# A fused state-space and feed-forward layer: the last 96 feed-forward features computed with tokens stationary

## The chip, the cores and the metric

The kernel runs on one core of a Trainium2 chip. The metric is the device time of one execution in microseconds. Engines are called by their profile names: PE (matrix multiplications), PEld (the loading of a stationary operand, shown beside PE), DVE (elementwise vector work), ACT (activation functions, also used for copies and scalings), POOL (small vector work), SP (here it only issues DMA transfers).

A multiplication on PE has a stationary operand (the kernel's `lhsT`, at most 128 contraction rows by 128 columns) and a moving operand (`rhs`, up to 512 columns here). The result has one partition for each stationary column and one element for each moving column. It goes to PSUM, which this kernel treats as eight banks of 128 partitions by 512 floats.

## The reference

`x` has 2048 tokens of 512 values. After a layer norm the same `xn` goes to two branches, whose outputs are added to `x`:

```python
xn = _layernorm(x)
# branch A: a diagonal complex recurrence over the tokens
dt = exp(log_dt); Lam_bar = exp(dt * Lam)
B_bar = ((Lam_bar - 1.0) / Lam)[:, None] * Bmat
Bu = einsum("bld,pd->blp", xn, B_bar)
h = Lam_bar * h + Bu[:, t, :]            # for each token t
yA = 2.0 * einsum("blp,dp->bld", hseq, Cmat).real + xn * Dskip
# branch B: a gated feed-forward layer, F = 1376 features
yB = (silu(xn @ w_gate) * (xn @ w_up)) @ w_down
out = x + yA + yB
```

F = 1376 is ten tiles of 128 features and one of 96. The change concerns this last tile of 96.

## The kernel before

**Chunks.** The 2048 tokens are worked in four chunks of 512, numbered 0 to 3. A chunk has these parts:

- Layer norm. Chunks 0 and 1 on DVE with a power on POOL (`ln_tile`), chunks 2 and 3 on ACT with a Newton iteration for the inverse square root on DVE (`ln_chunk_act`, four rounds of three small instructions, L550 to L552).
- `xnT`, the chunk with the 512 inputs on partitions: four token tiles of 128 by four input tiles. Chunk 0 is brought there by PE, chunks 1 to 3 by one DMA transposition each (`xTd1` to `xTd3`). There are two buffers, by `c % 2`.
- Gate and up products (`ffn_mm`, L760): for each of the eleven feature tiles four multiplications, one for each input tile. The weights are stationary (128 columns, 96 for the last tile), the 512 tokens move, so features come out on partitions. In chunk 0 the first six gate tiles are done in quarters of 128 tokens instead (L787). ACT takes the gate bank through SiLU into `sg` (L773, L812) and copies the up bank to `uf` (L824); DVE multiplies them into `hT` (L826), which is again stationary-ready: features on partitions, tokens along the row.
- State-space input products (`ssm_b_unit`, L840): four units, each of two banks filled by four multiplications; ACT copies them to `u_sb` (L847, L849); DVE rotates them, runs the scan and rotates back into `hss` (`ssm_elem_chunk`, L870 to L894).
- Down and output products (`dc_chunk`): four banks, one for 128 tokens each. Each first gets eleven multiplications of `hT` by `wd` (L925), then eight of `hss` by the prepared output weights `W12` (L938). Between these two groups PE does the input products of the chunk after next (the `mid` argument). DVE adds `x` (L945) and SP stores the result.

**Order.** PE and SP work strictly in the order in which the program adds their tasks. ACT, DVE and POOL get theirs from a list scheduler that runs while the kernel is built (`_schedule`), by estimated times and priorities, so their order can move when any task changes; on the chip each engine still works its list in order and waits on semaphores. PE's order is: quarters of chunk 0, the rest of the feed-forward part of chunk 0, input products of chunks 0 and 1, feed-forward part of chunk 1, down products of chunk 0, input products of chunk 2, output products of chunk 0, feed-forward part of chunk 2, and so on; chunk 3 has no further input products to put between.

**Banks.** `next_bank` gives out the bank whose last use is oldest.

**DMA order.** Nearly all transfers are issued by SP. A transposition waits for all transfers before it (in `dma`), and every ordinary transfer waits for the last transposition before it, so transpositions run alone. SP's order: the first tiles of `x`, the gate and up weights, four more tiles of `x`; then the transpositions of B (`ld_bre`, `ld_bim` into `BT`) and `xTd1`; then the last eight tiles of `x` and the skip vector `dsk` (`loads_x`); then the transpositions of C (into `hss[:, 1]`, which is free until chunk 1 needs it) and `wd` (`loads_stage_b2`); then `xTd2`, the stores of chunk 0, `xTd3`, and the other stores. `dsk` is used by `resid_chunk` (L617, L619).

Of the kernel before, what the change touches and what calls it, by code (L numbers as in the profile page):

```python
# [251 lines left out]
def bass_parallel_sum__ssm_conv_s5__swiglu_ffn__prompt_kernel(  # L252
# [32 lines left out]
    with es:  # L285
        block = es.enter_context(nc.Block())

        def sb(name, shape, dt):
            return es.enter_context(nc.sbuf_tensor(name, shape, dt))
# [8 lines left out]
        NXN = 8  # L298
        xn_sb = sb("xn_sb", [128, NXN, D], B16)
        xnT = sb("xnT", [128, 2, 4, KT, 128], B16)  # L300
        wg = sb("wg", [128, KT, Fh], B16)
        wu = sb("wu", [128, KT, Fh], B16)
        wd = sb("wd", [128, FT, D], B16)
        BT = sb("BT", [128, 2, KT, P], B16)
        W12 = sb("W12", [128, 2, PT, D], B16)
# [60 lines left out]
                return pb16[rows, b, cols]  # L366
        ptr = _PT()

        bank_ctr = [0]
        bank_state = {}  # L370

        def _bank_live(b):
            lw = g.last_w.get(("bk", b, 0))
            rd = g.readers.get(("bk", b, 0), ())
            return lw is not None and lw.eng == "pe" and len(rd) == 0 and not lw.name.startswith("pe_warm")

        bank_given = {}

        def next_bank():
            best = None  # L380
            for b in range(NB):
                if _bank_live(b):
                    continue
                key = max([bank_given.get(b, -1)] + [r.idx for h in range(2) for r in g.readers.get(("bk", b, h), ())])
                if best is None or key < best[0]:
                    best = (key, b)
            assert best is not None, "all PSUM banks live"
            bank_given[best[1]] = len(g.tasks)
            return best[1]

        next_tr = next_bank
# [12 lines left out]
        def dma(name, dst, src, writes, nbytes, reads=(), after=(), out_=False, eng="sp", xpose=False, prio=0.0, **kw):  # L404
            after = tuple(after)
            if xpose:
                after = after + tuple(dma_tasks)
                fn = lambda e, dst=dst, src=src: e.dma_start_transpose(out=dst, in_=src)
                est, nb = 2000.0, int(nbytes * 1.45)
            else:  # L410
                if xp_state[0] is not None:
                    after = after + (xp_state[0],)
                fn = lambda e, dst=dst, src=src: e.dma_start(dst, src, **kw)
                est, nb = 330.0 + nbytes / 900.0, nbytes
            t = g.add(eng, fn, reads=reads, writes=writes, name=name, dma=True, after=after, out=out_, est=est, nbytes=nb, prio=prio)
            dma_tasks.append(t)
            if xpose:
                xp_state[0] = t
            return t
# [19 lines left out]
        dma("ld_x4", x_sb[:, 4:8, :], x_v[:, 4:8, :], [("x", a) for a in range(4, 8)], 4 * TILEB)  # L439

        def loads_stage_b1():
            dma("ld_bre", BT[:, 0], A_B_re, [("BT", 0, kt) for kt in range(KT)], 512 * 512 * 2, xpose=True)
            dma("ld_bim", BT[:, 1], A_B_im, [("BT", 1, kt) for kt in range(KT)], 512 * 512 * 2, xpose=True)

        def loads_x():
            dma("ld_x8", x_sb[:, 8:12, :], x_v[:, 8:12, :], [("x", a) for a in range(8, 12)], 4 * TILEB)
            dma("ld_x12", x_sb[:, 12:16, :], x_v[:, 12:16, :], [("x", a) for a in range(12, 16)], 4 * TILEB)
            dma("ld_dsk", dsk[:], A_Dskip.partition_broadcast(128), [("dsk",)], 128 * 1024)

        def loads_stage_b2():  # L450
            dma("ld_cre", CT[:, 0], A_C_re, [("CT", 0)], 512 * 512 * 2, xpose=True)
# [10 lines left out]
              writes=[("iot",)], name="iota", est=1000)  # L462
        g.add("pool", lambda e: e.memset(halfpi[:], math.pi / 2.0), writes=[("halfpi",)], name="halfpi", est=100)
        g.add("pool", lambda e: e.memset(car[:, 0], 0.0), writes=[("car", 0)], name="car0", est=100)
        g.add("pool", lambda e: e.memset(ecst[:], math.e), writes=[("ecst",)], name="ecst", est=100)
        g.add("act", lambda e: e.activation(out=sm[:, NSM - 1, :], in_=mhalf[:, 0:PT], func=AF.Silu), reads=[("mhalf",)], writes=[("sm", "_warm")],
              name="act_warm", est=220, prio=1e6)
# [65 lines left out]
        def ln_chunk_act(c):  # L533
            A = range(4 * c, 4 * c + 4)
            cs = slice(4 * c, 4 * c + 4)
            for a in A:
                g.add("act", lambda e, a=a: e.activation(out=junk[:], in_=x_sb[:, a, :], func=AF.Identity, scale=-1.0 / D, accum_out=nmr[:, a:a + 1]),
                      reads=[("x", a)], writes=[("nmean", a), ("junk",)], name="lsum%d" % a, est=620)
                g.add("act", lambda e, a=a: e.activation(out=junk[:], in_=x_sb[:, a, :], func=AF.Square, bias=nmr[:, a:a + 1], accum_out=ve[:, a:a + 1]),
                      reads=[("x", a), ("nmean", a)], writes=[("ss", a), ("junk",)], name="lsq%d" % a, est=710)  # L540
            V, Y, T, M = ve[:, cs], rstd[:, cs], lnt[:, 0, :], nmr[:, cs]
            SS, V_, Y_, T_, NM = [("ss", a) for a in A], [("lv", c)], [("ly", c)], [("lt",)], [("nmean", a) for a in A]

            def d(nm, fn, rd, wr):
                g.add("dve", fn, reads=rd, writes=wr, name="%s%d" % (nm, c), est=75)
            d("lv", lambda e: e.tensor_scalar(out=V, in0=V, scalar1=1.0 / D, scalar2=EPS, op0=ALU.mult, op1=ALU.add), SS, V_)
            d("li", lambda e: e.tensor_scalar(out=T.bitcast(I32), in0=V.bitcast(I32), scalar1=1, scalar2=None, op0=ALU.logical_shift_right), V_, T_)
            d("ly", lambda e: e.tensor_scalar(out=Y.bitcast(I32), in0=T.bitcast(I32), scalar1=-1.0, scalar2=1597463007.0, op0=ALU.mult, op1=ALU.add), T_, Y_)
            for k in range(4):
                d("na%d" % k, lambda e: e.tensor_tensor(out=T, in0=Y, in1=Y, op=ALU.mult), Y_, T_)  # L550
                d("nb%d" % k, lambda e: e.scalar_tensor_tensor(out=T, in0=T, scalar=-0.5, in1=V, op0=ALU.mult, op1=ALU.mult), T_ + V_, T_)
                d("nc%d" % k, lambda e: e.scalar_tensor_tensor(out=Y, in0=T, scalar=1.5, in1=Y, op0=ALU.add, op1=ALU.mult), T_ + Y_, Y_)  # L552
            d("nm", lambda e: e.tensor_tensor(out=V, in0=M, in1=Y, op=ALU.mult), NM + Y_, V_)
            for a in A:
                g.add("act", lambda e, a=a: e.activation(out=xn_sb[:, a % NXN, :], in_=x_sb[:, a, :], func=AF.Identity, scale=rstd[:, a:a + 1], bias=ve[:, a:a + 1]),
                      reads=[("x", a)] + V_ + Y_, writes=[("xn", a % NXN)], name="xn%d" % a, est=620)

        def XN(c, j):
            return [("xnT", c % 2, j, 0), ("xnT", c % 2, j, 1)]
# [50 lines left out]
        def xt_chunk_dma(c):  # L610
            s0 = (4 * c) % NXN
            dma("xTd%d" % c, xnT[:, c % 2].rearrange("p j k t -> p (j k) t"), xn_sb[:, s0:s0 + 4, :],
                XNC(c), 4 * TILEB, reads=[("xn", s0 + j) for j in range(4)], xpose=True, prio=(_CFG["prio_xt"] if c > 1 else 0.0))
# [153 lines left out]
        def ffn_gate(c, i):  # L767
            fs = fsz[i]
            bk = ffn_mm(c, i, "g")
            sl = gctr[0] % NG  # L770
            gctr[0] += 1
            sg_slot[(c, i)] = sl
            g.add("act", lambda e, sl=sl, bk=bk, fs=fs: e.activation(out=sg[0:fs, sl, :], in_=pbank[0:fs, bk, :], func=AF.Silu),  # L773
                  reads=BK(bk), writes=[("sg", sl)], name="silu%d_%d" % (c, i), est=490)
# [40 lines left out]
        def ffn_up(c, i):  # L815
# [12 lines left out]
            else:  # L828
                g.add("dve", lambda e, sl=sl, bk=bk, fs=fs, i=i, hb=hb: e.tensor_tensor(out=hT[0:fs, hb, i, :], in0=sg[0:fs, sl, :], in1=pbank[0:fs, bk, :], op=ALU.mult),
                      reads=[("sg", sl)] + BK(bk), writes=[("hT", hb, i)], name="hmulp%d_%d" % (c, i), est=660, after=aH)  # L830

        usctr = [0]
        uctr = [0]

# [18 lines left out]
        def ssm_b_chunk(c):  # L853
            return [ssm_b_unit(c, pt) for pt in range(PT)]
# [101 lines left out]
        ln_chunk(1)  # L956
        loads_stage_b1()
        xt_chunk_dma(1)
        loads_x()
        loads_stage_b2()  # L960
        for i in range(0, 6):
            ffn_up(0, i)
        for i in range(6, FT):
            ffn_gate(0, i)
        for i in range(6, FT):
            ffn_up(0, i)
        units = []
        u0 = ssm_b_chunk(0)
# [4 lines left out]
            wprep_C(pt)  # L973
        u1 = ssm_b_chunk(1)
        ssm_elem_chunk(1, u1)
        for i in range(FT):
            ffn_gate(1, i)
            ffn_up(1, i)
        resid_chunk(1)
        ln_chunk(3)  # L980
        xt_chunk_dma(2)
        dc_chunk(0, mid=lambda: units.append(ssm_b_chunk(2)))
        ssm_elem_chunk(2, units[-1])
        for i in range(FT):
            ffn_gate(2, i)
            ffn_up(2, i)
        xt_chunk_dma(3)
        dc_chunk(1, mid=lambda: units.append(ssm_b_chunk(3)))
        ssm_elem_chunk(3, units[-1])
        for i in range(FT):  # L990
            ffn_gate(3, i)
            ffn_up(3, i)
        resid_chunk(2)
        resid_chunk(3)
        dc_chunk(2)
# [61 lines left out]
```

## Time and profile before

| what | value |
|---|---|
| median of 3 runs | 181.74 us (181.73 to 182.13) |
| the profiled execution, its own time | 181.75 us |
| its span, first to last instruction | 180.0 us |
| around the span | 1.75 us |
| granted PE clock | 1.0 throughout |
| multiplications, of all kinds | 910 |
| of these with 96 feature columns stationary (gate and up, last tile) | 32 |
| slowest engines by busy share | PE 98%, DVE 91%, ACT 57% |

The profile is of one execution. "Span" is the time from the first to the last instruction; the rest of the execution's time lies before and after. A busy PE in the page counts overlapping multiplications as one stretch, and the duration that the page gives for one multiplication includes the time to drain; the pace of a stream is read from the start of one group to the start of the next.

### The profile page before, as it was taken

To read this page: it belongs to the slowest core of one execution; us is meant where nothing else is said; L and a number is where in the kernel's file an instruction comes from. 1 tells how busy PE (TensorE), PEld (TensorE's weight loads), DVE (VectorE), ACT (ScalarE), POOL (GpSimd) and SP (SyncE) were. 2 spreads that over 40 slices of the span, in tenths; PEclk is the share of its full clock that TensorE was granted. 3 is DMA by queue.
4 is the path that set the end of the run, shared out by engine and by line. 5 is a ranking of instruction groups with operands and counts; after the bars stand their busy time and mean duration, and the time that the engine had idled before them with its cause. 6 is when DMAs were issued, how large, how long until landed. Compare 5 with 4: busy or idle time off the path is not lost.

```text
span 180.0 us, 2560 instructions
## 1 busy us (share of the span) xinstructions
PE 175.7 (98%) x910; PEld 85.0 (47%) x910; DVE 164.2 (91%) x354; ACT 101.7 (57%) x195; POOL 12.5 (7%) x34
## 2 busy tenths in 40 slices
PE   8899999999999999999999999999999999999994
PEld 3684444444444444444444544444444444444643
DVE  3797868999899889999999999999989999999993
ACT  3299989999999899872666600630666720000000
POOL 3531500000000610000000000000000000000000
PEclk9999999999999999999999999999999999999999
DMA  4994465666905300002340000002000000000112
GB/s 131 336 376 73 92 133 107 234 117 117 299 15 33 88 0 0 0 2 76 82 79 2 0 0 4 0 0 87 29 0 4 0 2 0 0 0 33 57 59 87
DMA packets 23396, 12.38 MB, mean 69 GB/s; under 512 B 15096, under 2 KB 23384, under 8 KB 23384
## 3 DMA queue, kind: packets, MB, share of 16 engines
q1 hardware_dynamic: 23360, 12.23, 26.0%
q8 instruction: 7, 0.11, 0.3%
q14 instruction: 5, 0.04, 0.1%
q10 hardware_dynamic: 24, 0.00, 0.0%
HBM read 6.46 MB, written 2.10 MB: 48 GB/s over the span
## 4 chain that ended last, share of the span: by engine, by line
PE 93%; DVE 2%; DMA 1%; POOL 1%; ACT 1%; issue 0%; DVEq 0%
PE pb L760 39%; PE pb L925 21%; PE pb L938 15%; PE pb L840 15%; PE pb L787 2%; DMA x_sb<-in_A_x_dram 1%; DVE st L505 1%; POOL rstd L511 1%; POOL sm L664 1%; ACT scrC L713 0%; DVE xn_sb L515 0%; DVE mv L507 0%; ACT xnT L606 0%; DVE osb L945 0%; DVE ve L509 0%
## 5 line engine op out<-in xcount | busy, mean ns | idle before, releaser
L760 PE MATMUL pb<-xnT,wu 128*128 128x512 bf16 (+1 forms) x176 | 43.7, 379 | 0.0
L879 DVE TENSOR_TENSOR_SCAN vq<-sm,car,vq 128x512 bf16<-128x512 f32 x32 | 39.5, 1270 | 0.1
L925 PE MATMUL pb<-wd,hT 128*128 128x512 bf16 (+3 forms) x187 | 38.7, 366 | 0.0
L760 PE MATMUL pb<-xnT,wg 128*128 128x512 bf16 (+1 forms) x152 | 38.4, 379 | 0.0
L773 ACT ACTIVATE sg<-pb 128x512 bf16<-128x512 f32 (+1 forms) x38 | 22.7, 596 | 15.3 <-PE pb L760 14.7
L824 ACT ACTIVATE uf<-pb 128x512 bf16<-128x512 f32 (+1 forms) x44 | 26.0, 603 | 7.3 <-PE pb L760 5.7
L938 PE MATMUL pb<-W,hss 128*128 128x512 bf16 (+1 forms) x136 | 28.3, 366 | 0.0
L840 PE MATMUL pb<-xnT,BT 128*128 128x512 bf16 x128 | 28.1, 379 | 0.0
L925 PEld LDWEIGHTS pb<-wd,hT 128*128 128x128 bf16 (+1 forms) x187 | 18.3, 98 | 19.9
L760 PEld LDWEIGHTS pb<-xnT,wu 128*128 128x128 bf16 (+1 forms) x176 | 17.6, 100 | 20.1
L760 PEld LDWEIGHTS pb<-xnT,wg 128*128 128x128 bf16 (+1 forms) x152 | 15.3, 101 | 17.6
L938 PEld LDWEIGHTS pb<-W,hss 128*128 128x128 bf16 x136 | 13.3, 98 | 14.4
L826 DVE TENSOR_TENSOR hT<-sg,uf 128x512 bf16<-128x512 bf16 (+1 forms) x44 | 18.1, 416 | 1.9 <-ACT uf L824 1.4
L840 PEld LDWEIGHTS pb<-xnT,BT 128*128 128x128 bf16 x128 | 12.5, 98 | 15.1
L847 ACT ACTIVATE u_sb<-pb 128x512 bf16<-128x512 f32 x16 | 9.5, 596 | 11.1 <-PE pb L840 10.7
L945 DVE TENSOR_TENSOR osb<-pb,x_sb 128x512 bf16<-128x512 f32 (+1 forms) x17 | 11.1, 655 | 1.5 <-PE pb L938 1.3
L870 DVE TENSOR_TENSOR scrA<-u_sb,cosT 128x1024 bf16<-128x1024 bf16 x16 | 10.9, 681 | 0.8 <-ACT u_sb L849 0.8
L885 DVE TENSOR_TENSOR scrA<-vq,cosT 128x1024 bf16<-128x1024 bf16 x16 | 11.0, 685 | 0.0
L889 DVE TENSOR_TENSOR scrA<-vq,sin 128x1024 bf16<-128x1024 bf16 x16 | 10.9, 684 | 0.0
L873 DVE TENSOR_TENSOR scrA<-u_sb,sin 128x1024 bf16<-128x1024 bf16 x16 | 10.9, 684 | 0.0
L875 DVE TENSOR_TENSOR vq<-scrA 128x1024 bf16<-128x1024 bf16 x16 | 10.5, 684 | 0.1
L894 DVE TENSOR_TENSOR hss<-scrA 128x1024 bf16<-128x1024 bf16 x16 | 10.4, 684 | 0.0
(79 smaller groups left out, 135.2 us busy)
## 6 DMA issues: line engine op xcount, KB each, us to landing
out_dram<-osb SPq DMA_DIRECT2D x15, 128.0 KB, 1.7
x_sb<-in_A_x_dram SPq DMA_DIRECT2D x3, 512.0 KB, 4.7
wd<-in_B_w_down_dram SPq DMA_DIRECT2D x1, 1280.0 KB, 6.8
wg<-in_B_w_gate_dram SPq DMA_DIRECT2D x2, 384.0 KB, 4.3
wu<-in_B_w_up_dram SPq DMA_DIRECT2D x1, 768.0 KB, 6.5
wg<-in_B_w_gate_dram SPq DMA_DIRECT2D x1, 608.0 KB, 7.6
wu<-in_B_w_up_dram SPq DMA_DIRECT2D x1, 608.0 KB, 8.7
x_sb<-in_A_x_dram SPq DMA_DIRECT2D x4, 128.0 KB, 2.8
```

The lines of the kernel that those rows point to most:

```text
L760: inst = e.matmul(pbank[0:fs, bk, :].rearrange("p (j t) -> p j t", j=4), lhsT=w[:, kt, i * 128:i * 128 + fs], rhs=xnT[:, c % 2, :, kt, :], ...
L773: g.add("act", lambda e, sl=sl, bk=bk, fs=fs: e.activation(out=sg[0:fs, sl, :], in_=pbank[0:fs, bk, :], func=AF.Silu), reads=BK(bk), write ...
L824: g.add("act", lambda e, ul=ul, bk=bk, fs=fs: e.activation(out=uf[0:fs, ul, :], in_=pbank[0:fs, bk, :], func=AF.Identity), reads=BK(bk), w ...
L826: g.add("dve", lambda e, sl=sl, ul=ul, fs=fs, i=i, hb=hb: e.tensor_tensor(out=hT[0:fs, hb, i, :], in0=sg[0:fs, sl, :], in1=uf[0:fs, ul, :] ...
L840: inst = e.matmul(pbank[:, bk, :].rearrange("p (j t) -> p j t", j=4), lhsT=BT[:, ri, kt, pt * 128:(pt + 1) * 128], rhs=xnT[:, c % 2, :, kt ...
L870: g.add("dve", lambda e, sl=sl, U=U, Cb=Cb: e.tensor_tensor(out=pr2[:, sl, 0], in0=U, in1=Cb, op=ALU.mult), reads=ru + rdt, writes=[("pr", ...
L873: g.add("dve", lambda e, sl=sl, Usw=Usw, S2=S2: e.tensor_tensor(out=pr2[:, sl, 1], in0=Usw, in1=S2, op=ALU.mult), reads=ru + rdt, writes=[ ...
L879: g.add("dve", lambda e, sl=sl, ri=ri, pt=pt, rr=rr, c=c: e.tensor_tensor_scan(out=vq[:, sl, 1, ri, :], data0=rr[:, pt:pt + 1].to_broadcas ...
L885: g.add("dve", lambda e, sl=sl, Q=Q, Cb=Cb: e.tensor_tensor(out=po2[:, sl, 0], in0=Q, in1=Cb, op=ALU.mult), reads=rq + rdt, writes=[("po", ...
L925: inst = e.matmul(pbank[:, bk, 0:nc_], lhsT=hT[0:fs, hb, i, lt * 128:(lt + 1) * 128], rhs=wd[0:fs, i, c0:c0 + nc_], start=(i == 0), stop=F ...
L938: inst = e.matmul(pbank[:, bk, 0:nc_], lhsT=hss[:, hb, pt, ri, lt * 128:(lt + 1) * 128], rhs=W12[:, ri, pt, c0:c0 + nc_], start=False, sto ...
L945: g.add("dve", lambda e, bk=bk, a=a, os_=os_, c0=c0, nc_=nc_: e.tensor_tensor(out=osb[:, os_, 0:nc_], in0=pbank[:, bk, 0:nc_], in1=x_sb[:, ...
```

## The change

The last tile of 96 gate and 96 up features is no longer computed by `ffn_mm`. A new function `ffn_rem` does it, once for each chunk: for each of the four token tiles, `xnT` (128 tokens) is the stationary operand, and the 96 gate columns and 96 up columns move together as 192 columns; for this the two weight tensors are now halves of one (`wgu`). Two token tiles share a bank, so the four fill two neighbouring banks, which `next_bank(2)` now can give. ACT makes SiLU of the gate columns of both banks in one instruction and copies the up columns in another; DVE multiplies them into `hr`, with tokens on partitions. A DMA transposition (`hr_dma`) then brings `hr` into its place in `hT`. `hr` has 128 columns for each token tile, of which 96 are written; all of it is set to zero once at the start by POOL.

In chunk 0 `ffn_rem` stands between the up tiles 0 to 5 and the gate tiles 6 to 9; in the other chunks it stands first in the feed-forward part. On SP, the transposition of chunk 0 stands after `xTd1` and before the last tiles of `x`; that of chunk 1 after `xTd2`; that of chunk 2 after `xTd3`; that of chunk 3 after the stores of chunk 1.

Two further edits: `dsk` is loaded ahead of the transpositions of B, and the Newton iteration of the layer norm has three rounds in place of four.

```diff
-        wg = sb("wg", [128, KT, Fh], B16)
-        wu = sb("wu", [128, KT, Fh], B16)
+        wgu = sb("wgu", [128, 2, KT, Fh], B16)
+        wg, wu = wgu[:, 0], wgu[:, 1]
+        FR = (FT - 1) * 128
+        NR = Fh - FR
+        hr = sb("hr", [128, 2, 4, 128], B16)
...
-        def next_bank():
+        def next_bank(width=1):
             best = None
-            for b in range(NB):
-                if _bank_live(b):
+            for b in range(NB - width + 1):
+                ages = [_bank_age(b + k) for k in range(width)]
+                if any(x is None for x in ages):
                     continue
...
         def loads_stage_b1():
+            dma("ld_dsk", dsk[:], A_Dskip.partition_broadcast(128), [("dsk",)], 128 * 1024)
...
         def loads_x():
...
-            dma("ld_dsk", dsk[:], A_Dskip.partition_broadcast(128), [("dsk",)], 128 * 1024)
...
+        g.add("pool", lambda e: e.memset(hr[:], 0.0), writes=[("hr0",)], name="hr0", est=400)
...
-            for k in range(4):
+            for k in range(3):
                 d("na%d" % k, ...
...
+        def ffn_rem(c):
+            ba = next_bank(2)
+            bb = ba + 1
+            for h, bk in enumerate((ba, bb)):
+                def mm(e, bk=bk, h=h):
+                    for l2 in range(2):
+                        for kt in range(KT):
+                            inst = e.matmul(pbank[:, bk, l2 * 256:l2 * 256 + 2 * NR].rearrange("p (w f) -> p w f", w=2), lhsT=xnT[:, c % 2, 2 * h + l2, kt, :],
+                                            rhs=wgu[:, :, kt, FR:Fh], start=(kt == 0), stop=(kt == KT - 1))
+                    return inst
+                g.add("pe", mm, reads=[("wg", 1), ("wu", 1)] + XN(c, 2 * h) + XN(c, 2 * h + 1), writes=BK(bk), name="mm_r%d_%d" % (c, h), est=8 * 84, ninst=8)
...
+            g.add("act", lambda e: e.activation(out=dst(sg[:, sl, :]), in_=src(0), func=AF.Silu), reads=BK(ba) + BK(bb), writes=[("sg", sl)], name="silur%d" % c, est=400)
+            g.add("act", lambda e: e.activation(out=dst(uf[:, ul, :]), in_=src(1), func=AF.Identity), reads=BK(ba) + BK(bb), writes=[("uf", ul)], name="uevr%d" % c, est=400)
+            hb = c % 2
+            g.add("dve", lambda e: e.tensor_tensor(out=dst(hr[:, hb].rearrange("p l f -> p (l f)")), in0=dst(sg[:, sl, :]), in1=dst(uf[:, ul, :]), op=ALU.mult),
+                  reads=[("sg", sl), ("uf", ul), ("hr0",)], writes=[("hr", hb)], name="hmulr%d" % c, est=300)
+
+        def hr_dma(c):
+            hb = c % 2
+            dma("hrT%d" % c, hT[:, hb, FT - 1, :].rearrange("p (j t) -> p j t", j=4), hr[:, hb], [("hT", hb, FT - 1)], 128 * 128 * 4 * 2, reads=[("hr", hb)], xpose=True)
...
+        FL = FT - 1
+        for i in range(0, 6):
+            ffn_up(0, i)
+        ffn_rem(0)
+        hr_dma(0)
         loads_x()
         loads_stage_b2()
-        for i in range(0, 6):
-            ffn_up(0, i)
-        for i in range(6, FT):
+        for i in range(6, FL):
             ffn_gate(0, i)
-        for i in range(6, FT):
+        for i in range(6, FL):
             ffn_up(0, i)
...
+        def ffn(c):
+            ffn_rem(c)
+            for i in range(FL):
+                ffn_gate(c, i)
+                ffn_up(c, i)
+        ffn(1)
...
         xt_chunk_dma(2)
+        hr_dma(1)
...
+        ffn(2)
         xt_chunk_dma(3)
+        hr_dma(2)
...
+        ffn(3)
+        hr_dma(3)
```

More of the change, by code (lines that the diff above doesn't have):

```diff
@@ L367, in bass_parallel_sum__ssm_conv_s5__swiglu_ffn__prompt_kernel @@
         ptr = _PT()
-        bank_ctr = [0]
         bank_state = {}
@@ L377, in bass_parallel_sum__ssm_conv_s5__swiglu_ffn__prompt_kernel, with _bank_age @@
         bank_given = {}
-        def next_bank():
+        def _bank_age(b):
+            if _bank_live(b):
+                return None
+            return max([bank_given.get(b, -1)] + [r.idx for h in range(2) for r in g.readers.get(("bk", b, h), ())])
+        def next_bank(width=1):
             best = None
-            for b in range(NB):
-                if _bank_live(b):
+            for b in range(NB - width + 1):
+                ages = [_bank_age(b + k) for k in range(width)]
+                if any(x is None for x in ages):
                     continue
-                key = max([bank_given.get(b, -1)] + [r.idx for h in range(2) for r in g.readers.get(("bk", b, h), ())])
-                if best is None or key < best[0]:
-                    best = (key, b)
+                if best is None or max(ages) < best[0]:
+                    best = (max(ages), b)
             assert best is not None, "all PSUM banks live"
-            bank_given[best[1]] = len(g.tasks)
+            for k in range(width):
+                bank_given[best[1] + k] = len(g.tasks)
             return best[1]
@@ L830, in ffn_up, with src, dst @@
                       reads=[("sg", sl)] + BK(bk), writes=[("hT", hb, i)], name="hmulp%d_%d" % (c, i), est=660, after=aH)
+        def ffn_rem(c):
[9 more added lines that the diff above has]
+                g.add("pe", mm, reads=[("wg", 1), ("wu", 1)] + XN(c, 2 * h) + XN(c, 2 * h + 1), writes=BK(bk), name="mm_r%d_%d" % (c, h), est=8 * 84, ninst=8)
+            sl = gctr[0] % NG
+            gctr[0] += 1
+            ul = uctr_f[0] % NUF
+            uctr_f[0] += 1
+            pf = pb16[:].bitcast(F32)
+            def src(w):
+                v = pf[:, ba:bb + 1, :].rearrange("p b (l f) -> p b l f", l=2)
+                return v[:, :, :, w * NR:(w + 1) * NR]
+            def dst(t):
+                return t.rearrange("p (b l f) -> p b l f", b=2, l=2)[:, :, :, 0:NR]
+            g.add("act", lambda e: e.activation(out=dst(sg[:, sl, :]), in_=src(0), func=AF.Silu), reads=BK(ba) + BK(bb), writes=[("sg", sl)], name="silur%d" % c, est=400)
[6 more added lines that the diff above has]
+            dma("hrT%d" % c, hT[:, hb, FT - 1, :].rearrange("p (j t) -> p j t", j=4), hr[:, hb], [("hT", hb, FT - 1)], 128 * 128 * 4 * 2, reads=[("hr", hb)], xpose=True)
         usctr = [0]
@@ L975, in bass_parallel_sum__ssm_conv_s5__swiglu_ffn__prompt_kernel @@
         ssm_elem_chunk(1, u1)
-        for i in range(FT):
-            ffn_gate(1, i)
-            ffn_up(1, i)
+        def ffn(c):
[4 more added lines that the diff above has]
+        ffn(1)
         resid_chunk(1)
@@ L981, in bass_parallel_sum__ssm_conv_s5__swiglu_ffn__prompt_kernel @@
         xt_chunk_dma(2)
+        hr_dma(1)
         dc_chunk(0, mid=lambda: units.append(ssm_b_chunk(2)))
         ssm_elem_chunk(2, units[-1])
-        for i in range(FT):
-            ffn_gate(2, i)
-            ffn_up(2, i)
+        ffn(2)
         xt_chunk_dma(3)
+        hr_dma(2)
         dc_chunk(1, mid=lambda: units.append(ssm_b_chunk(3)))
         ssm_elem_chunk(3, units[-1])
-        for i in range(FT):
-            ffn_gate(3, i)
-            ffn_up(3, i)
+        ffn(3)
+        hr_dma(3)
         resid_chunk(2)
```

## The prediction

> **What bounds the kernel now.** I read the engine totals first, then the chain of waits, then the stages it runs through. PE is busy for 98% of the span; DVE, with 91%, is close behind.
>
> ```profile
> PE 175.7 (98%) x910; PEld 85.0 (47%) x910; DVE 164.2 (91%) x354; ACT 101.7 (57%) x195; POOL 12.5 (7%) x34
> ```
>
> The chain that ended last (start, length, engine and line, all in us) shows that from 10.44 us to 177.46 us there is nothing on it but PE, group after group without a gap. In the list of waits PE has three entries, 1.6 us together, all in the head of the kernel.
>
> ```profile
> 10.44 2.85 PE pb L787 x48
> 13.29 13.81 PE pb L760 x64
> 27.10 13.81 PE pb L840 x64
> 40.91 18.99 PE pb L760 x88
> 59.91 9.51 PE pb L925 x44
> 69.42 6.91 PE pb L840 x32
> ...
> 170.52 6.94 PE pb L938 x40
> 177.46 0.03 issue
> 177.49 0.02 DVEq L246
> 177.51 0.04 issue
> 177.55 0.42 DVE osb L945
> ```
>
> So a nanosecond taken from PE's stream is a nanosecond of the result, as long as no other engine starts to hold PE up; and everything off PE counts only through its lead.
>
> **PE: removed and added.** 64 multiplications of 512 columns take 13.81 us: 215.8 ns each. Those with 96 stationary columns move 512 tokens like the rest (379 ns in the page, the same as with 128), so a 96-wide tile pays the price of a 128-wide one. Removed per chunk: 8 x 215.8 = 1726 ns. Added per chunk: 16 multiplications of 192 columns. No row has 192, but the timeline of PE (start, length, ...) has a stream of 128 columns, each with a new stationary operand of 128 columns, as the new ones have:
>
> ```profile
> 10.44 2.85 PE L787 MATMUL pb<-xnT,wg 128*128 128x128 bf16 x48
> 13.12 1.24 PE L760 MATMUL pb<-xnT,wu 128*128 128x512 bf16 x5
> ```
>
> From start to start 48 take 2.68 us: 55.8 ns each. The line through (128, 55.8) and (512, 215.8) gives 0.417 ns a column and 82.5 ns at 192. The last stage has a third size: of the 40 in 6.94 us, 24 are of 512 and 16 of 256 columns, so (6940 - 24 x 215.8) / 16 = 110 ns, where the line gives 109. Added: 16 x 82.5 = 1320 ns. Net per chunk -406 ns, for four chunks -1.62 us.
>
> Could the weight load set the pace, now that 16 loads replace 8?
>
> ```profile
> L787 PEld LDWEIGHTS pb<-xnT,wg 128*128 128x128 bf16 x96 | 5.5, 98 | 0.9 <-ACT xnT L606 0.5 <-issue 0.4
> L760 PEld LDWEIGHTS pb<-xnT,wg 128*96 128x96 bf16 x16 | 2.0, 123 | 1.6
> ```
>
> A load of 128 columns lasts 98 ns, but at 55.8 ns per pair it is evidently overlapped. Bounds for the pace: 80 ns (192 x 0.417, no fixed part) and 98 ns (a load at full length each time). I take 82.5, since the nearest row, with the same loads and a shorter stream, is not held by them. The upper bound would leave 1726 - 1568 = 158 ns a chunk, 0.6 us in all.
>
> A rule speaks against the change. The Trainium skill, "TensorE: Matmul & The Clock Gate", section "Back-to-back issue gap", says that load-and-multiply pairs in real kernels sustain about 81 ns at 128 columns and about 131 ns at 512. An estimate from that page, 89 ns at 192 on the line between, makes 16 x 89 - 8 x 131 = +0.38 us a chunk and a result 1.5 us slower. This trace contradicts both of its figures, 55.8 and 215.8, and the measurement decides.
>
> **ACT and DVE.** Per chunk, ACT's two instructions and DVE's product keep their number but shrink from 512 to 384 elements a partition; at most they stay as long (0.60, 0.60 and 0.42 us in the page). Three Newton rounds for four remove 3 instructions in chunks 2 and 3, at 0.195 us from start to start: 1.2 us of DVE. On the path: nothing, since PE never waits for DVE here. DVE's smallest lead is at the end: the last two `hss` products end at 166.94 and PE wants them at 170.52.
>
> ```profile
> 165.65 1.29 DVE L894 TENSOR_TENSOR hss<-scrA 128x1024 bf16<-128x1024 bf16 x2
> ```
>
> 3.6 us of lead; PE gains 1.6 us against DVE, which itself loses 1.2 us and the shorter products. That cover holds.
>
> **POOL.** The clearing of `hr`, 1024 elements, stands before the iota. From 128 columns in 0.20 us and a tiny one in 0.10 it is worth some 0.9 us; POOL then idles 2.12 us before its first power at 4.16. Nothing on the path; if it took 3 us, the head would start 0.9 us later.
>
> **SP: what is moved and added.** This is where the change can lose.
>
> ```profile
> 20.57 1.95 SPq L408 DMA_TRANSPOSE BT<-in_A_B_im_dram  x1
> 24.89 1.76 SPq L408 DMA_TRANSPOSE xnT<-xn_sb  x1
> 29.58 0.93 SPq L413 DMA_DIRECT2D x_sb<-in_A_x_dram  x2
> 30.54 0.50 SPq L413 DMA_DIRECT2D dsk<-in_A_Dskip_dram  x1
> 35.06 1.95 SPq L408 DMA_TRANSPOSE hss<-in_A_C_re_dram  x1
> 39.52 2.12 SPq L408 DMA_TRANSPOSE hss<-in_A_C_im_dram  x1
> 44.10 1.03 SPq L413 DMA_DIRECT2D wd<-in_B_w_down_dram  x2
> 55.97 2.91 SPq L408 DMA_TRANSPOSE xnT<-xn_sb  x1
> ```
>
> `dsk` leaves a later group and is put before the B transpositions: at most its issue, 0.50 us, later for these and `xTd1`, and as much is given back behind. PE wants the second half of B one bank (0.86 us) after 27.10 and it is there by 24.89: 3.1 us of lead, 2.2 after the 0.50 and PE's own 0.41 us in chunk 0.
>
> The new transposition `hrT0` of 128 KB puts a full stop into SP's queue. Its price, issue to landing: not under 1.5 us (the quickest store, 64 KB), not over 5.5 us (the slowest transposition, four times the data). I take 2.8 us, the median of plain 128 KB loads. It needs no wait for data: `hr` of chunk 0 is ready near 23 us, `xTd1` lands at 29.5. Queued behind it, all later by 2.8 (1.5 to 5.5) us:
>
> - `x` tiles 8 to 11, for ACT's sums of chunk 2. ACT read them at 33.67 before; its new list has this read after four more bank evacuations, the last of a bank that PE completes 11 x 0.86 us after it starts the input products at 26.7, so at 36.2, and the read comes at 36.8. The load landed by 33.7 at the latest, so 36.5 now: in time. At 5.5 us ACT would stand 2.4 us with evacuations behind it; PE reuses a bank only 8 x 0.86 = 6.9 us later there, so it doesn't notice yet.
> - C lands at 47 to 50 instead of 44.1; ACT first uses it at 63.36.
> - `wd`: issued at 44.10 with 6.8 us to landing, so 51, and 54 to 56.5 after; PE wants it at 59.91 - 0.81 = 59.1.
> - `xTd2` waits for ACT's normalised tiles at 55.97 anyway, hardly later; PE wants it 0.8 us before 69.42, and it lands by 61.
>
> The three other `hrT` land tens of microseconds ahead: that of chunk 3 is issued near 127 and wanted near 159. With 2.8 us nothing of this reaches PE.
>
> **Sum.** Four chunks x -0.406 = -1.62 us on PE, all else 0. Span 180.0 - 1.6 = 178.4, plus 1.75 around it = 180.1 us; the profiled execution's 181.75 is the median's 181.74, so no correction: **180.1 us**.
>
> **Rivals.**
> (1) PE is shortened, but part of it is given back: by a pace of up to 98 ns (+1.0 us) or a short stall where ACT's cushion is thinnest. That place is the third input unit of chunk 2: four of eight banks are then held by half-done down products, so PE comes back to a bank after four. The second bank is evacuated at 72.25 and refilled from 73.74, 1.5 us of cushion. For it: ACT is busy 18.55 of 19.0 us in 40.9 to 59.9, so a delay taken at 36 us is hardly worked off. Against: all rows used. Time 180.6 to 181.6, say 181.0.
> (2) The slower side: `hrT0` blocks SP much longer than any transposition here. ACT waits for `x` tile 8, and the delay arrives at that thin place. It begins to cost PE at 2.8 + 0.3 + 1.5 us plus some 1.2 us that ACT idles in between, about 6 us, and then 1 us for each 1 us; it outweighs the gain by 0.5 us from about 8.2 us on. At 9 us: 180.1 + 3 = 183.1. For it: a transposition inside SBUF of small pieces is unlike the loads; against: `xTd` is the same kind with four times the data and takes 4.3 to 5.1 us.
> (3) The change doesn't do what it says, because DVE with 91% takes over as the bound and the end stays: 181.7. DVE is full from 83 to 112 us (19.00 of 19.00, then 9.50 of 9.50). Against: the lead of 3.6 us above, and its own work shrinks.
>
> **How the numbers follow.** Forecast 0.72; partly given back 0.14 (most of it still faster); slower 0.07; no gain 0.07. A measurement of this kernel tells about 0.3% from no change, 0.55 us. Faster than 181.2: 0.72 + 0.11 = 0.83; within 0.3%: 0.03 + 0.06 = 0.09; slower: 0.08. The range goes from 179.8 (pace of 80 ns, 0.16 us, and some scatter) up to 181.1, which takes in the 98 ns pace and most of rival 1.
>
> **What would show it.** Right: 64 multiplications of 192 columns, 16 from start to start in about 1.32 us; no wait of PE after 11 us; feed-forward stages of chunks 1 to 3 of 18.6 instead of 19.0 us. SP: `hrT0` landing 2 to 4 us after issue. Wrong: a pace near 100 ns or more; a wait of PE on ACT in the third input unit of chunk 2, with ACT waiting for `x` near 37 us; or an end of the chain on DVE.

## The result and the profile after

| | before | after |
|---|---|---|
| median of 6 runs each | 181.79 us (181.73 to 182.13) | 180.18 us (180.09 to 180.70) |
| ratio to before, 95% interval | | 0.9913 [0.9898, 0.9928] |
| profiled execution, its own time / its span | 181.75 / 180.0 us | 180.45 / 178.6 us |
| multiplications | 910 | 942 |

The kernel became 0.9% faster: 1.61 us by the medians, where 1.6 had been forecast (180.1 us). The interval does not reach 1.

The first lines of the changed kernel's page give the span and each engine's busy time, share and instructions:

```profile
span 178.6 us, 2625 instructions
PE 174.9 (98%) x942; PEld 86.8 (49%) x942; DVE 162.1 (91%) x348; ACT 98.9 (55%) x195; POOL 13.1 (7%) x35
```

PE is still full, with 32 instructions more. The chain of waits of the changed kernel (start, length, what) shows how its stages now lie:

```profile
13.34 5.18 PE pb L769 x24
18.52 1.32 PE pb L848 x16
19.84 6.91 PE pb L769 x32
26.75 13.81 PE pb L882 x64
40.56 1.32 PE pb L848 x16
41.88 17.27 PE pb L769 x80
59.15 9.51 PE pb L967 x44
68.66 4.32 PE pb L882 x20
72.98 0.03 issue
73.01 2.76 PE pb L882 x12
...
169.15 6.94 PE pb L980 x40
176.09 0.02 issue
176.11 0.42 DVE osb L987
```

L848 is the new remainder: 16 multiplications of 192 columns in 1.32 us, 82.5 ns each. With the 80 that follow it the feed-forward stage of a chunk takes 18.59 us, where it took 18.99. Everything else has the length that it had. One place is not gapless: the input products of chunk 2 (L882), 32 in 6.91 us before, are broken after 20, and the last 12 take 2.76 us where 12 x 0.216 would be 2.59. That is the place that the prediction had called the thinnest.

Two views of the changed kernel show why. The first is ACT's timeline (start, length, ..., and in brackets the idle time before it and what ended it), the second SP's:

```profile
36.57 0.66 ACT L889 ACTIVATE u_sb<-pb 128x512 bf16<-128x512 f32 x1
38.85 0.63 ACT L546 ACTIVATE junk<-x_sb 128x512 bf16<-128x512 bf16 x1 [1.62 <-DMA x_sb<-in_A_x_dram]
39.39 0.19 ACT L546 ACTIVATION_READ_ACCUMULATOR junk<-x_sb 128x1 f32 x1
39.48 0.58 ACT L891 ACTIVATE u_sb<-pb 128x512 bf16<-128x512 f32 x1
...
72.37 0.58 ACT L891 ACTIVATE u_sb<-pb 128x512 bf16<-128x512 f32 x1
```

```profile
7.05 2.35 SPq L421 DMA_DIRECT2D dsk<-in_A_Dskip_dram  x1
17.45 2.02 SPq L416 DMA_TRANSPOSE BT<-in_A_B_re_dram  x1
22.23 2.25 SPq L416 DMA_TRANSPOSE BT<-in_A_B_im_dram  x1
26.56 3.38 SPq L416 DMA_TRANSPOSE xnT<-xn_sb  x1
32.84 1.19 SPq L416 DMA_TRANSPOSE hT<-hr  x1
35.26 0.93 SPq L421 DMA_DIRECT2D x_sb<-in_A_x_dram  x2
```

ACT stands 1.62 us for the `x` tiles of chunk 2, with bank evacuations behind it. The last line is the evacuation on which the multiplications at 73.01 wait: it ends at 72.95, where it ended at 72.25 before. SP issued the `x` tiles at 35.26 us, against 29.58 before: 2.4 us of it is the new transposition (32.84 to 35.26), the other 3.3 were there before it. The first B transposition was issued 2.4 us later (17.45 against 15.08); 1.7 of that is left when `xTd1` is issued (26.56 against 24.89). And from the issue of `xTd1` to the next one 6.3 us pass, where it was 4.7.

```profile
15.08 2.57 SPq L408 DMA_TRANSPOSE BT<-in_A_B_re_dram  x1
```

That line is the first B transposition in the kernel before.

### The profile page after: what moved, and what is told of

Same layout as the page of the kernel before. It is cut to its first block, busy times and chain, and to the rows that moved or that the text cites. A ratio compares the mean times of both kernels' runs of the same rounds, so it can differ in the third digit from the quotient of the medians.

```text
span 178.6 us, 2625 instructions
## 1 busy us (share of the span) xinstructions
PE 174.9 (98%) x942; PEld 86.8 (49%) x942; DVE 162.1 (91%) x348; ACT 98.9 (55%) x195; POOL 13.1 (7%) x35
## 4 chain that ended last, share of the span: by engine, by line
PE 93%; DVE 2%; POOL 1%; DMA 1%; ACT 1%; issue 0%
PE pb L769 36%; PE pb L967 21%; PE pb L882 16%; PE pb L980 15%; PE pb L848 3%; PE pb L796 2%; DMA x_sb<-in_A_x_dram 1%; DVE st L514 1%; POOL rstd L520 1%; POOL sm L673 1%; ACT scrC L722 0%; DVE xn_sb L524 0%; DVE mv L516 0%; ACT xnT L615 0%; DVE osb L987 0%
## 5 line engine op out<-in xcount | busy, mean ns | idle before, releaser
L769 PE MATMUL pb<-xnT,wgu 128*128 128x512 bf16 x296 | 64.7, 379 | 0.0
L769 PEld LDWEIGHTS pb<-xnT,wgu 128*128 128x128 bf16 x296 | 28.9, 98 | 33.8
L833 ACT ACTIVATE uf<-pb 128x512 bf16<-128x512 f32 x40 | 24.4, 618 | 8.2 <-PE pb L769 5.3
L882 PE MATMUL pb<-xnT,BT 128*128 128x512 bf16 x128 | 28.3, 379 | 0.0
L782 ACT ACTIVATE sg<-pb 128x512 bf16<-128x512 f32 x34 | 20.7, 614 | 4.0 <-PE pb L769 4.0
L882 PEld LDWEIGHTS pb<-xnT,BT 128*128 128x128 bf16 x128 | 12.4, 98 | 15.5 <-ACT u_sb L891 0.8
L835 DVE TENSOR_TENSOR hT<-sg,uf 128x512 bf16<-128x512 bf16 x40 | 16.0, 414 | 0.1
L889 ACT ACTIVATE u_sb<-pb 128x512 bf16<-128x512 f32 x16 | 9.8, 611 | 10.5 <-PE pb L882 10.5
L891 ACT ACTIVATE u_sb<-pb 128x512 bf16<-128x512 f32 x16 | 9.6, 600 | 1.1 <-PE pb L882 1.1
L514 DVE BATCH_NORM_STATS2 st<-x_sb 128x6 f32<-128x512 bf16 x8 | 5.2, 684 | 5.5 <-DMA x_sb<-in_A_x_dram 5.5
```

Of the source, the lines that this page charges most:

```text
L769: inst = e.matmul(pbank[0:fs, bk, :].rearrange("p (j t) -> p j t", j=4), lhsT=w[:, kt, i * 128:i * 128 + fs], rhs=xnT[:, c % 2, :, kt, :], ...
L833: g.add("act", lambda e, ul=ul, bk=bk, fs=fs: e.activation(out=uf[0:fs, ul, :], in_=pbank[0:fs, bk, :], func=AF.Identity), reads=BK(bk), w ...
L835: g.add("dve", lambda e, sl=sl, ul=ul, fs=fs, i=i, hb=hb: e.tensor_tensor(out=hT[0:fs, hb, i, :], in0=sg[0:fs, sl, :], in1=uf[0:fs, ul, :] ...
L882: inst = e.matmul(pbank[:, bk, :].rearrange("p (j t) -> p j t", j=4), lhsT=BT[:, ri, kt, pt * 128:(pt + 1) * 128], rhs=xnT[:, c % 2, :, kt ...
```

## The experiments

There is one theory, A, and there are four rivals. A: the gain is PE's shorter stream and nothing else; the other edits and the DMA work are worth nothing as long as their cushions hold. Rivals: B, part of the gain comes from DVE's relief and the early `dsk`; C, SP's stop costs something in every run; D, the weight load sets the pace; E, the banks absorb any delay on SP. The ratios are to runs of the kernel before that were taken in the same series (medians 181.78 and 181.80 us). Beside each run's time stands one number that the noise of the first loads doesn't touch: the stretch on PE from the start of the first 512-column multiplication to PE's end. It was 164.32 us before and 162.90 after.

**Put `dsk` back.**

```diff
         def loads_stage_b1():
-            dma("ld_dsk", dsk[:], A_Dskip.partition_broadcast(128), [("dsk",)], 128 * 1024)
...
             dma("ld_x12", x_sb[:, 12:16, :], x_v[:, 12:16, :], [("x", a) for a in range(12, 16)], 4 * TILEB)
+            dma("ld_dsk", dsk[:], A_Dskip.partition_broadcast(128), [("dsk",)], 128 * 1024)
```

> The changed kernel with the load of dsk put back behind the last x tiles. Theory A (the whole gain is PE's shorter stream, the other edits are worth nothing on the path): 180.1 us, a ratio to before of 0.991. Theory A also holds that the early dsk held up the first transposition of B by 2.4 us (issued at 17.45 instead of 15.08), so here it is issued near 15.1, ACT's wait for x tile 8 (1.62 us in the changed kernel) disappears or falls under 0.3 us, and PE has no wait after 11 us. Rival B (the early dsk frees DVE earlier and part of the gain comes from that): 180.5 us or more. The list of ACT and DVE may shift a little, since the scheduler sees another DMA order.

Measured: 180.21 us, ratio 0.9886 [0.9862, 0.9911]. The stretch on PE is 162.69 us without a wait, and ACT doesn't wait for `x`. So rival B has nothing here. But the first transposition of B was issued at 16.23, not near 15.1, although `dsk` was no longer ahead of it. Its time of issue in all profiles was 16.23, 15.02 and 15.08 with the late `dsk`, and 17.45, 16.22, 15.62, 16.94, 16.64, 16.05 and 15.11 with the early one (means 15.4 and 16.3). The scatter of the first loads is as large as the difference, so that `dsk` caused the 2.4 us isn't shown. Whether it costs some tenths stays open; on PE it could tell only by way of the `x` tiles, as in the profile above.

**`dsk` early and three Newton rounds, no change to the remainder.** The kernel before with

```diff
         def loads_stage_b1():
+            dma("ld_dsk", dsk[:], A_Dskip.partition_broadcast(128), [("dsk",)], 128 * 1024)
...
-            dma("ld_dsk", dsk[:], A_Dskip.partition_broadcast(128), [("dsk",)], 128 * 1024)
...
-            for k in range(4):
+            for k in range(3):
```

> The kernel before with two of the three edits alone: dsk loaded early and three Newton rounds; the last 96 features stay with the weights stationary. Theory A: PE's stream is unchanged, so 181.8 us, within 0.2 us of before, though DVE's busy time falls by about 1.2 us. Rival B (DVE, 91% busy, sets the end, or the early dsk helps): 180.6 to 181.2 us.

Measured: 181.83 us, ratio 1.0001 [0.9983, 1.0020]; the stretch on PE 164.32 us, as before. The engine totals of this run:

```profile
PE 175.7 (98%) x902; PEld 85.1 (47%) x910; DVE 163.5 (91%) x348; ACT 101.8 (57%) x195; POOL 12.9 (7%) x34
```

DVE has six instructions less (348 for 354), and the end didn't move. Rival B falls. (902 of 910 multiplications: eight records are missing from this trace.)

**The transposition of chunk 0 later on SP.**

```diff
         ffn_rem(0)
-        hr_dma(0)
         loads_x()
         loads_stage_b2()
+        hr_dma(0)
```

> The changed kernel with the transposition of chunk 0's remainder moved on SP behind the loads of C and wd. Theory A: nothing after it waits for it any more, x tile 8 lands about 2.4 us sooner (near 36.5), ACT's wait for it vanishes, and PE waits nowhere after 11 us; the time is 180.1 us as in the changed kernel, at most 0.2 us less, because the third input unit of chunk 2 no longer comes late (0.2 us in the profile of the changed kernel). Rival C (the stop that the transposition puts into SP's queue costs as much as 0.5 us in typical runs): 179.6 us.

Measured: 180.84 us (180.40 to 181.71), ratio 0.9930 [0.9902, 0.9957]; the stretch on PE 162.69 us, no wait in it. By the stretch theory A is right. The median is 0.7 us higher than expected. In the profiled execution, the fastest of the six, PE waited 0.4 us in the head, before 11 us, for the gate weights, which this edit doesn't touch. The spans of the six go from 178.4 to 179.7 us (178.3 to 178.9 in the six of the changed kernel), so most of the excess lies inside the span; the other five have no profile, and where in the span it lies stays open. ACT's wait for `x` didn't vanish but was 0.8 us, since the list scheduler, seeing the load earlier, put ACT's read two units earlier (34.30 instead of 38.85): the expectation had that wrong. Rival C's 179.6 didn't appear.

**Gate and up columns multiplied apart.** The inner loop of `ffn_rem`:

```diff
-                        for kt in range(KT):
-                            inst = e.matmul(pbank[:, bk, l2 * 256:l2 * 256 + 2 * NR].rearrange("p (w f) -> p w f", w=2), lhsT=xnT[:, c % 2, 2 * h + l2, kt, :],
-                                            rhs=wgu[:, :, kt, FR:Fh], start=(kt == 0), stop=(kt == KT - 1))
+                        for w in range(2):
+                            for kt in range(KT):
+                                inst = e.matmul(pbank[:, bk, l2 * 256 + w * NR:l2 * 256 + (w + 1) * NR], lhsT=xnT[:, c % 2, 2 * h + l2, kt, :],
+                                                rhs=wgu[:, w, kt, FR:Fh], start=(kt == 0), stop=(kt == KT - 1))
```

> The changed kernel with gate and up columns of the remainder multiplied apart: 32 multiplications of 96 columns per chunk in place of 16 of 192, each with its own load of 128 stationary columns. Theory A by the line 0.417 ns a column plus 2.5 ns: 42.5 ns each, 1.36 us a chunk in place of 1.32, so 180.3 us. Rival D (under some length the weight load sets the pace; 55.8 ns per load is the fastest that a profile here has shown, 98 ns is what one load lasts): 55.8 ns would give 1.79 us a chunk and 182.0 us, 98 ns would give 3.14 us a chunk and 187.4 us.

Measured: 180.51 us, ratio 0.9915 [0.9889, 0.9941]. The chain, and the groups of its remainder (busy us, mean ns, idle before):

```profile
82.61 1.36 PE pb L849 x32
```

```profile
L849 PE MATMUL pb<-wgu,xnT 128*128 128x96 bf16 x128 | 6.1, 206 | 0.0
L849 PEld LDWEIGHTS pb<-wgu,xnT 128*128 128x128 bf16 x128 | 5.9, 98 | 0.9
```

1.36 us / 32 = 42.5 ns, exactly on the line, although a load is still recorded with 98 ns. The stretch on PE is 162.85 us: 0.16 us more than 162.69, which is 64 extra multiplications at 2.5 ns. So rival D falls, for streams down to 96 columns: a load of 128 columns was sustained every 42.5 ns. Shorter streams were not run.

**The transposition of chunk 0 three and five times.** The repeats are hidden from the list scheduler's clock (an edit of their estimated times, not shown), so that PE, ACT, DVE and POOL have instruction for instruction the order of the changed kernel:

```diff
         hr_dma(0)
+        for _ in range(2):       # 4 in the second kernel
+            hr_dma_again(0)
         loads_x()
```

> The changed kernel with chunk 0's transposition done three times on SP, each waiting for the one before; the order of work on PE, ACT, DVE and POOL is instruction for instruction that of the changed kernel. Each repeat takes 2.4 us, so the last x tiles are issued 4.8 us later: near 36 us where the first loads land as early as in the split run (31.16 there), near 40 where they land as late as in the profile of the changed kernel (35.26 there). Theory A with the cushion of the prediction (the changed kernel loses nothing as long as these tiles are issued before about 35.3 us, and from there on 1 us for each 1 us): 180.8 us with early first loads, up to 185 with late ones, all of it lost at the third input unit of chunk 2. Rival E (banks and slots absorb such a delay, SP's queue doesn't matter): 180.2 us.

> The same with five times: the last x tiles are issued 9.6 us later than in the changed kernel, near 41 us with early first loads. Theory A: 180.1 + (41 - 35.3) = 185.8 us, 4.8 us more than with three (or 5.0, if that run was still in part inside the cushion), slower than the kernel before. PE's wait is at the third input unit of chunk 2, with a smaller one possible in the feed-forward part of chunk 1. Rival E: 180.2 to 181 us.

Measured: three times, 183.52 us (182.05 to 184.57), ratio 1.0073 [1.0033, 1.0113]; five times, 189.10 us (187.94 to 189.52), ratio 1.0390 [1.0355, 1.0426]. SP, ACT and PE of the kernel with three (timelines):

```profile
31.85 6.03 SPq L416 DMA_TRANSPOSE hT<-hr  x3
39.10 0.93 SPq L421 DMA_DIRECT2D x_sb<-in_A_x_dram  x2
```

```profile
42.65 0.63 ACT L546 ACTIVATE junk<-x_sb 128x512 bf16<-128x512 bf16 x1 [5.86 <-DMA x_sb<-in_A_x_dram]
```

```profile
43.91 4.49 PE L769 MATMUL pb<-xnT,wgu 128*128 128x512 bf16 x20 [1.25 <-ACT u_sb L896]
48.64 12.26 PE L769 MATMUL pb<-xnT,wgu 128*128 128x512 bf16 x56 [0.23 <-ACT uf L865]
...
75.80 3.86 PE L887 MATMUL pb<-xnT,BT 128*128 128x512 bf16 x16 [1.93 <-ACT u_sb L894]
```

The `x` tiles were issued at 39.10, that is 3.8 us past the point (35.3 us) at which the prediction's cushion ends, and the profiled execution's stretch on PE is 166.87 us, 4.2 us longer than 162.69. With five, issue at 44.20: 8.9 us past it, and a stretch of 171.85 us, 9.2 us longer. So theory A's 1 us for 1 us holds, and rival E falls. The 185.8 us expected with five was for an issue near 41 us; from 44.20 the theory makes 189.0. The place was wrong: part of the loss comes earlier, in the feed-forward stage of chunk 1. With three, PE's losses from start to start are 1.4 and 0.4 us there and 2.3 us at the third input unit of chunk 2. With five, the largest part is one wait in the feed-forward stage; slow multiplications behind it make up most of the rest (see the last section), and 0.1 us is left for the third input unit:

```profile
44.20 0.94 SPq L421 DMA_DIRECT2D x_sb<-in_A_x_dram  x2
```

```profile
47.82 0.63 ACT L546 ACTIVATE junk<-x_sb 128x512 bf16<-128x512 bf16 x1 [10.85 <-DMA x_sb<-in_A_x_dram]
```

```profile
49.08 7.11 PE L769 MATMUL pb<-xnT,wgu 128*128 128x512 bf16 x20 [6.24 <-ACT u_sb L896]
```

What sets the loss is ACT's list: from its read of the `x` tiles (42.65 and 47.82) for the next 37 us each of its instructions stands 5.16 to 5.17 us later with five than with three.

**Both moves on SP.** `dsk` back and the transposition of chunk 0 behind C and `wd`, the edits of the first and third experiment together.

> The changed kernel with both moves on SP: dsk back behind the last x tiles, and chunk 0's transposition behind C and wd. ACT's and DVE's lists shift a little. Theory A: PE's stream is the same, so 180.1 us, no wait of PE after 11 us, the stretch from the first 512-column multiplication to the end of PE as short as in the other variants without such a wait (162.7 us). Rival C (SP's stop costs something in typical runs): 179.6 us.

Measured: 180.44 us (179.97 to 180.53), ratio 0.9919 [0.9904, 0.9934]; the stretch on PE 162.69 us without a wait.

**The changed kernel again.**

> The changed kernel again, unaltered, on the same chip as the other three, for comparison. Theory A: 180.2 us; its 0.2 us at the third input unit of chunk 2 appears only if the first loads land late, that is, if the first transposition of B is issued after about 17 us. If the early dsk were what holds that transposition up, it would be issued near 17.4 again.

Measured: 180.48 us (180.24 to 180.80), ratio 0.9928 [0.9912, 0.9943], the first transposition of B issued at 16.05, the `x` tiles at 33.73, no wait of PE after the head, and a stretch of 162.69 us. In it the evacuation that PE waited for above ends at 71.65, not 72.95:

```profile
71.07 0.58 ACT L891 ACTIVATE u_sb<-pb 128x512 bf16<-128x512 f32 x1
```

Counted from the start of the stretch (13.55 here, 13.18 there) it comes 1.7 us sooner, about the 1.62 us that ACT had stood there. So the 0.2 us at the third input unit in the profile above belongs to an execution whose `x` tiles came late. Four kernels with the same PE stream (this one, `dsk` back, transposition late, both) agree in the stretch to 0.01 us, while their medians spread over 180.2 to 180.8: what differs between their profiled spans lies before it, since the stretch starts anywhere from 13.05 to 13.86 us. In three of the four PE waits for the gate weights in the head, 0.4 to 1.0 us, with `dsk` in either place. The time around the span differs too (2.0 to 2.3 us). What spreads the medians is not shown beyond that. None of the variants is faster than the changed kernel by more than this spread.

## Why the prediction was right

- *Removed and added on PE*: 1726 - 1320 = 406 ns a chunk. The chain shows 1.32 us a chunk, and 164.32 - 162.69 = 1.63 us in all, against 1.62 forecast. The price of 192 columns, which no row had, came from a line through two others, and the split kernel put a third point on it (96 columns, 42.5 ns).
- *The rule that spoke against it* gives 81 ns at 128 columns and 131 at 512 (the Trainium skill, "TensorE: Matmul & The Clock Gate", section "Back-to-back issue gap"). It does not hold here: these runs have 42.5, 55.8, 82.5 and 215.8 ns at 96, 128, 192 and 512 columns, with a new stationary operand each time.
- *ACT, DVE and POOL cost nothing on the path*: shown for DVE by the run without the new remainder. ACT's two new instructions take 0.49 us each, not 0.60; POOL's clearing 0.95 us, forecast 0.9, in its idle time.
- *The price of `hrT0`*: 2.8 us taken, 1.5 to 5.5 as bounds; measured 2.4 (median of four, one of 4.1).
- *`dsk`, at most 0.50 us later for B*: in the profile the first B transposition was 2.4 us later than before, and in other runs up to 1.2 us with `dsk` late and up to 1.9 us with it early. The term was sized by one issue and left out the scatter of the first loads, which moves SP's whole queue.
- *`x` tile 8 in time, at 36.5 for a read at 36.8*: it missed by 1.6 us in the profile, because of that scatter and a longer `xTd1`, and was just in time in the changed kernel's other profile (read at 37.26). The short stall of the first rival was real, and its size 0.2 us in one of the two profiles; its pace of up to 98 ns did not come. What kept the loss so small is the cushion of 1.5 us at that place, which the prediction had counted. The 0.3 us by which the `x` tiles were to be in time is less than the scatter of the loads: where they were in time, it was luck.
- *The cushion of about 6 us for SP, then 1 us for 1 us*: confirmed in size by three and five repeats (3.8 past it gave 4.2, 8.9 gave 9.2). The place was only half right: the feed-forward stage of chunk 1 gives way too, and with five it gives way first and most.
- *DVE as the new bound*: fell. Its last `hss` products end at 162.48 and PE wants them at 169.15, a lead of 6.7 us where it was 3.6.

## What to carry to other kernels

Where one matrix dimension leaves a remainder, let it move instead of stand: in these runs a stationary tile of 96 cost as much PE time as one of 128 (215.8 ns for 512 columns), while moving columns were paid one by one, down to the 96 that were tried, and the swap pays if the result can be brought back in place off the path. Price a missing size by a line through sizes that the profile has. And look for the price of such a change not on the engine that it relieves but in the queue that gets the new work: find what stands behind it, and by how much it may be late.

## What the hardware showed unasked

After the long wait in the kernel with five transpositions PE was slow for a while. Three stretches of that run (start and end, length, busy time and instructions of PE, PEld, DVE, ACT and POOL, then the granted clock, DMA share, GB/s):

```profile
43.00:49.00 6.00, 0.00 (x0) 0.00 (x0) 0.00 (x0) 1.18 (x4) 0.00 (x0) 0.88 0.64 195
49.10:54.30 5.20, 5.20 (x13) 1.89 (x14) 0.53 (x3) 5.20 (x14) 0.00 (x0) 0.50 0.56 101
54.50:60.00 5.50, 5.50 (x27) 2.53 (x26) 5.45 (x9) 5.50 (x15) 0.00 (x0) 1.00 0.55 101
```

After 6.2 us without a multiplication the granted clock was 0.50 for about 5.4 us more, and the 13 multiplications from 49.08 on took 5.4 us from start to start, where 13 x 0.216 is 2.8: 2.6 us of PE's time. They added nothing to the run's 9.2 us: ACT's list kept its 5.16 us against the kernel with three all through them, and PE still had to wait 0.1 us for it at the third input unit. At full clock PE would have waited there for about 2.7 us instead (an estimate: 0.1 + 2.6). Waits of 1.3 and 1.9 us in the kernel with three left the clock at 1.00. The Trainium skill, "TensorE: Matmul & The Clock Gate", section "What's actually happening", has the clock halved after an idle window of about 3.4 us, which agrees with both sides here; it has full clock back after at least one busy window of about 3.4 us, and here it took 5.4.
